# Four matmuls of 128 columns and two levels of sums in place of four matmuls of 256 columns and one level, in the inverse stage of a spectral block

## The chip, the cores and the metric

One core of a Trainium2 chip. The metric is the device time of the whole program in microseconds (us), on the slowest core, which here is the only one. In the profiles PE is TensorE's matmul, PEld its weight load, DVE VectorE, ACT ScalarE, POOL GpSimd and SP the queue that issues loads and stores.

## The reference, cut to what matters

```python
# A: normalise rows, 2-D real FFT (2048 x 512), multiply by W, inverse FFT
h  = x + irfft2(rfft2(layernorm(x)) * (w_r + 1j * w_i))
# B: normalise again, squared-ReLU MLP (512 -> 1792 -> 512), residual
r  = relu(layernorm(h) @ w1 + b1)
h2 = h + (r * r) @ w2 + b2
```

The 2048 rows lie as 16 groups of 128. The transforms are matmuls with sine and cosine tables. The change touches the last transform, which turns 257 complex frequencies into the 512 columns of a group.

## The kernel before: the parts that the change touches

For a group g, `s5` makes the even part of the output (256 columns of the table for lt = 0 and 2) and the odd part (lt = 1 and 3). `s5b` adds and subtracts them to the 512 columns R, by the symmetry of sine and cosine about the middle. `s6` multiplies by the row transform KI. `s6a` and `s6b` add x and take row statistics. Comments are mine.

```python
def s5(g, ahead=False):
    pe = bank("p5", "po", 2) if ahead else bank("p5", "pp", 3)
    for e in range(2):
        for r in range(2):
            lt = 2 * r + e
            nc.tensor.matmul(pe[:, 256 - 256 * e:512 - 256 * e],
                             lhsT=T2[:, lt, g].rearrange("p q s -> p (q s)"),
                             rhs=GI[:, lt, :], start=(r == 0), stop=(r == 1))
    def rest():
        od = ffn.tile([P, 256], FP32, tag="od", bufs=4, name="od")
        nc.scalar.copy(od[:], pe[:, 256:512])        # ACT: one half of PSUM to SBUF
        Rs[g] = pe, od
    ...
def s5b(g):                                          # DVE: two adds of 256 fp32, one side PSUM
    pe, od = Rs[g]
    Rs[g] = R = ffn.tile([P, 512], BF16, tag="R", bufs=3, name="R")
    nc.vector.tensor_tensor(R[:, 0:256], pe[:, 0:256], od[:], ALU.add)
    nc.vector.tensor_tensor(R[:, 256:512], pe[:, 0:256], od[:], ALU.subtract)
```

The groups are normalised and sent through the MLP in five chunks. While the MLP of chunk c runs ("loop c"), the pieces of chunk c+1 are dealt between its slots. A slot is one `up` of four matmuls or one `down` of four or five. Which slot a piece follows is decided when the program is built, by a counter of estimated PE time:

```python
CHUNKS = ((0, 2), (2, 5), (5, 9), (9, 13), (13, 16))

def prep_steps(c, total):                            # pieces of chunk c: (time, cost, piece)
    ...
        if k >= 2:
            steps.append((t, 0.22, lambda g=a + k - 2: s6(g)))
        if k < n:
            steps.append((t, 0.44, lambda g=a + k: s5(g)))
        if 1 <= k <= n:
            steps.append((t + 0.1, 0, lambda g=a + k - 1: s5b(g)))
        if k >= 2:
            steps.append((t + 0.1, 0, lambda g=a + k - 2: (s6a(g), s6b(g, on_act(c, g)))))
    t = t0 + (n + 1) * gap
    steps.append((t + 1.6, 0, lambda: rstd(c)))
    steps.append((t + 2.2, 0, lambda: norm(c)))
    steps.append((total - 2.4, 0.12 * n, lambda: transp(c, 0)))
    steps.append((total - 1.7, 0.12 * n, lambda: transp(c, 1)))

def run(c):
    ...
        prep = prep_steps(c + 1, sum(t for t, _ in slots) + 0.9 * n)
    for k, (t, slot) in enumerate(slots):
        slot()
        at += t
        while prep and (prep[0][0] <= at or k == len(slots) - 1):
            _, cost, piece = prep.pop(0)
            piece()
            at += cost
```

The 0.9 a group is 0.44 (s5) + 0.22 (s6) + 0.24 (transposes). Every engine then keeps this order.

## Time and profile before

| | before |
|---|---|
| time, median of 3 | 172.66 us (172.52 to 172.68) |
| span of the profiled run | 170.8 us |
| PE busy | 157.6 us, 92% |
| DVE busy | 123.6 us, 72% |
| ACT busy | 106.3 us, 62% |
| s5 in the loops | 4 x 256 columns, 0.44 us of PE a group |
| s5b in the loops | 2 adds, 0.66 us of DVE a group from start to start |

### The profile page before, as it was taken

How to read it: one execution, taken by the hardware profiler on the slowest of the kernel's cores; microseconds unless marked ns; L12 is line 12 of the kernel's file. 1: busy time of each engine (PE TensorE's matmuls, PEld its weight loads, DVE VectorE, ACT ScalarE, POOL GpSimd, SP SyncE). 2: the span in 40 equal slices, each digit the busy share in tenths (PEclk: the TensorE clock that was granted, in tenths of full speed). 3: DMA queues.
4: the chain of work that ended last, by engine and by line, in shares of the span. 5: the costliest groups of instructions: out<-in, count | busy, mean ns of one | idle time of the engine just before them, and what ended most of it. 6: DMA issues, size and time to landing. Idle time of an engine off the chain costs nothing.

```text
span 170.8 us, 2709 instructions
## 1 busy us (share of the span) xinstructions
PE 157.6 (92%) x967; PEld 92.4 (54%) x981; DVE 123.6 (72%) x287; ACT 106.3 (62%) x188; POOL 36.7 (22%) x63
## 2 busy tenths in 40 slices
PE   3988797999989899899999999999999999999992
PEld 1455565887854774456445444544544454556461
DVE  6998678979956698668997577498567577578320
ACT  3999785898976772288653677245387434478200
POOL 7788900000000003134000235000034200025000
PEclk9999999999999999999999999999999999999999
DMA  5994999992000000100000100000100001010011
GB/s 165 326 281 83 223 152 272 387 241 26 0 0 0 4 0 2 55 12 0 0 31 31 35 0 2 0 31 31 35 30 0 0 31 33 25 38 0 0 60 34
DMA packets 12621, 11.42 MB, mean 67 GB/s; under 512 B 6976, under 2 KB 11072, under 8 KB 12608
## 3 DMA queue, kind: packets, MB, share of 16 engines
q1 hardware_dynamic: 12448, 10.33, 22.6%
q0 software_dynamic: 160, 0.92, 1.9%
q8 instruction: 7, 0.11, 0.3%
q14 instruction: 6, 0.05, 0.1%
HBM read 8.01 MB, written 2.10 MB: 59 GB/s over the span
## 4 chain that ended last, share of the span: by engine, by line
PE 72%; DVE 16%; ACT 5%; issue 2%; POOL 2%; DVEq 0%; POOLq 0%; ACTq 0%
PE ph L688 29%; PE po L721 25%; DVE st L215 3%; PE p L542 3%; PE p L344 3%; ACT U L361 2%; PE po L709 2%; PE p L643 2%; PE p L587 1%; PE idle L259 1%; POOL rs L222 1%; DVE KFr L226 1%; DVE mA L419 1%; ACT X L391 1%; DVE mB L419 1%
## 5 line engine op out<-in xcount | busy, mean ns | idle before, releaser
L688 PE MATMUL ph<-UT,W 128*128 128x384 bf16 (+2 forms) x278 | 49.8, 336 | 1.6 <-DVE UT L774 0.6
L691 ACT ACTIVATE rl<-ph,b1f 128x384 bf16<-128x384 f32 (+2 forms) x70 | 41.5, 602 | 13.7 <-PE ph L688 10.6
L721 PE MATMUL po<-W,act 128*128 128x512 bf16 x203 | 48.1, 379 | 0.4
L692 DVE TENSOR_TENSOR act<-rl 128x384 bf16<-128x384 bf16 (+2 forms) x70 | 34.2, 514 | 15.4 <-ACT rl L691 14.9
L688 PEld LDWEIGHTS <-W 128*128 128x128 bf16 x280 | 27.3, 98 | 22.9 <-issue 2.1
L695 POOL TENSOR_TENSOR hb<-hs,b2b 128x512 f32<-128x512 bf16 x16 | 18.4, 1153 | 98.2 <-DVE act L692 98.2
L721 PEld LDWEIGHTS <-act 128*128 128x128 bf16 x210 | 20.4, 98 | 21.8
L725 DVE TENSOR_TENSOR ot<-po,hb 128x512 bf16<-128x512 f32 x15 | 10.3, 688 | 9.3 <-PE po L721 8.0
L591 DVE SCALAR_TENSOR_TENSOR hs<-p,xs 128x512 bf16<-128x512 f32 x15 | 10.3, 684 | 1.2 <-PE p L587 0.9
L259 PE MATMUL p<-ones 128*128 128x512 bf16 x22 | 8.1, 516 | 2.9 <-POOL ones L152 2.9
L546 ACT COPY od<-p 128x256 f32<-128x256 f32 x14 | 5.1, 370 | 7.9 <-PE p L542 7.9
L647 ACT COPY UT<-p 128x768 bf16<-128x768 bf16 (+1 forms) x4 | 3.6, 906 | 9.4 <-PE p L643 9.4
L542 PE MATMUL p<-GI,T 128*128 128x256 bf16 x56 | 8.2, 272 | 0.4 <-DVE hs L591 0.2
L259 PEld LDWEIGHTS <-ones 128*128 128x128 bf16 x40 | 4.4, 112 | 7.6 <-POOL ones L152 2.9
L602 ACT ACTIVATE junk<-hs 128x512 bf16<-128x512 bf16 x6 | 3.8, 630 | 7.6 <-DVE hs L591 7.6
L344 PE MATMUL p<-GF,Bt 128*128 128x256 bf16 x64 | 8.3, 273 | 0.0
L577 DVE TENSOR_TENSOR R<-p,od 128x256 bf16<-128x256 f32 x15 | 6.2, 415 | 2.4 <-ACT od L561 1.3
L215 DVE BATCH_NORM_STATS2 st<-xs 128x6 f32<-128x512 bf16 x12 | 7.8, 676 | 0.0
L542 PEld LDWEIGHTS <-T 128*128 128x128 bf16 x56 | 5.4, 97 | 3.5 <-issue 1.2
L473 ACT CAST T<-p 128x1024 bf16<-128x1024 f32 x7 | 7.2, 1025 | 0.0
L344 PEld LDWEIGHTS <-Bt 128*128 128x128 bf16 x64 | 6.1, 98 | 1.4 <-DVE Bt L251 0.4
L605 DVE BATCH_NORM_STATS2 st<-hs 128x6 f32<-128x512 bf16 x9 | 6.3, 695 | 0.3
(177 smaller groups left out, 226.0 us busy)
## 6 DMA issues: line engine op xcount, KB each, us to landing
W<-in_B_w_dram SPq DMA_DIRECT2D x2, 1792.0 KB, 10.3
out_dram<-ot SPq DMA_DIRECT2D x15, 128.0 KB, 1.8
xs<-in_A_x_dram SPq DMA_DIRECT2D x3, 512.0 KB, 6.5
WB<-in_A_w_r_dram SPq DMA_DIRECT2D x1, 578.2 KB, 6.0
WB<-in_A_w_i_dram SPq DMA_DIRECT2D x1, 578.2 KB, 7.2
xs<-in_A_x_dram SPq DMA_DIRECT2D x2, 256.0 KB, 3.3
b2b<-in_B_b_dram SPq DMA_DIRECT2D x1, 128.0 KB, 8.7
out_dram<-ot SPq DMA_DIRECT2D x2, 64.0 KB, 1.9
```

Source lines behind the costliest of these rows:

```text
L215: nc.vector.bn_stats(st[:], xs[:, g, :])
L259: nc.tensor.matmul(o, lhsT=ones[:, 0:P], rhs=ones[:], start=True, stop=True)
L344: nc.tensor.matmul(puv[:, :, e, :], lhsT=Bt[:, 2 * t + 1 - e, 2 * pr + q, :], rhs=GFv[:, t, :, e, :], start=(t == 0), stop=(t == 1))
L473: nc.scalar.copy(dst, src[0])
L542: nc.tensor.matmul(pe[:, 256 - 256 * e:512 - 256 * e], lhsT=T2[:, lt, g].rearrange("p q s -> p (q s)"), rhs=GI[:, lt, :], start=(r == 0), ...
L591: nc.vector.scalar_tensor_tensor(hs[:, g, :], Ys.pop(g)[:], WSC, xs[:, g, :], ALU.mult, ALU.add)
L688: nc.tensor.matmul(ph[:, 0:n], lhsT=W1[:, d, bass.ts(f, P)], rhs=UT[:, d, 0:n], start=(d == 0), stop=(d == ND - 1))
L691: nc.scalar.activation(rl[:, 0:n], ph[:, 0:n], ACT.Relu, bias=b1f[:, f:f + 1], scale=1.0)
L692: sq = nc.vector.tensor_tensor(act[:, f, 0:n], rl[:, 0:n], rl[:, 0:n], ALU.mult)
L695: add = nc.gpsimd.tensor_tensor(hb[:, g, :], hs[:, g, :], b2b[:], ALU.add)
L721: nc.tensor.matmul(po[:], lhsT=act[:, f, bass.ts(i, P)], rhs=W2[:, f, :], start=(f == 0), stop=(f == NF - 1))
L725: nc.vector.tensor_tensor(ot[:], po[:], hb[:, g, :], ALU.add)
```

## The change

The intent is to halve the PE work of `s5`. Sine and cosine are symmetric once more about the quarter, so 128 columns of each of the four tables are enough. They are no longer accumulated but kept apart, and a first level of sums on DVE (H) makes the even and odd parts. ACT copies all 512 columns to bfloat16 (V), and the four columns without a partner (two of each part) to H. Groups 0 and 1, which come first, keep their old way. The table gets 128 more columns. The counter charges 0.22 for s5. One of the two copies made ahead moves into loop 0.

```diff
     def s5(g, ahead=False):
-        for e in range(2):
-            for r in range(2):
-                lt = 2 * r + e
-                nc.tensor.matmul(pe[:, 256 - 256 * e:512 - 256 * e], lhsT=T2[:, lt, g]..., rhs=GI[:, lt, :],
-                                 start=(r == 0), stop=(r == 1))
+        for lt, tb, o in ((1, GI[:, 1, 0:129], 0), (3, GI[:, 3, 1:128], 129), (0, GI[:, 0, 0:128], 256),
+                          (2, GIa[:, 1024:1152], 384)):
+            nc.tensor.matmul(pe[:, o:o + tb.shape[1]], lhsT=T2[:, lt, g]..., rhs=tb, start=True, stop=True)
         def rest():
-            nc.scalar.copy(od[:], pe[:, 256:512])
-            Rs[g] = pe, od
+            nc.scalar.copy(V[:].rearrange("p e h c -> p (e h c)"), pe[:])
+            nc.scalar.copy(H[:, :, 0:129:128], pe[:]...[:, :, :, 0])
+            Rs[g] = V, H
     def s5b(g):
+        nc.vector.tensor_tensor(H[:, :, 1:128], V[:, :, 0, 1:128], V[:, :, 1, 1:128], ALU.add)
+        nc.vector.tensor_tensor(H[:, :, 255:128:-1], V[:, :, 0, 1:128], V[:, :, 1, 1:128], ALU.subtract)
+        nc.vector.tensor_tensor(Rv[:, 0::3], he, ho, ALU.add)
+        nc.vector.tensor_tensor(Rv[:, 2:0:-1], he, ho, ALU.subtract)
@@ prep_steps
-        steps = []
+        steps = [(0.4, 0, rest[1])] if c == 1 else []
-                steps.append((t, 0.44, lambda g=a + k: s5(g)))
+                steps.append((t, 0.22, lambda g=a + k: s5(g)))
... (the tiles V and H, three buffers each; group 0's old sums; the wider table GIa and its angles;
     rest[0] before the first transposes: cut)
```

The total of 0.9 a group in `run` was left as it was.

More of the change, by code (lines that the diff above doesn't have):

```diff
@@ L80 @@
     KI = persist.tile([P, P], BF16, name="KI")
-    GI = persist.tile([P, 4, 256], BF16, name="GI")
+    GIa = persist.tile([P, 1152], BF16, name="GIa")
+    GI = GIa[:, 0:1024].rearrange("p (t c) -> p t c", t=4)
     GIn = persist.tile([P, 2, 256], BF16, name="GIn")
@@ L140 @@
     fiE = [tab.tile([P, 9 * P], I32, name=f"fiE{i}") for i in range(2)]
-    fiI = tab.tile([P, 1024], I32, name="fiI")
+    fiI = tab.tile([P, 1152], I32, name="fiI")
     nc.gpsimd.iota(pI[:, 0:1], pattern=[[0, 1]], base=0, channel_multiplier=1)
@@ L327 @@
                                 float(HT if lt // 2 else QT), ALU.mult, ALU.add)
+    nc.gpsimd.memset(idxD[:, 0:1], 384)
+    nc.gpsimd.tensor_scalar(fiI[:, 1024:1152], idxD[:, 0:P], cols[:, 4:5], float(HT), ALU.mult, ALU.add)
     def cos_negs():
@@ L511 @@
         if pr == 5:
-            sin_of(GI[:].rearrange("p t c -> p (t c)"), fiI[:])
-            nc.scalar.activation(GIn[:], fiI[:].bitcast(I16)[:, ::2].rearrange("p (t c) -> p t c", t=4)[:, 0::2, :],
+            sin_of(GIa[:], fiI[:])
+            nc.scalar.activation(GIn[:], fiI[:, 0:1024].bitcast(I16)[:, ::2].rearrange("p (t c) -> p t c", t=4)[:, 0::2, :],
                                  ACT.Sin, scale=-SIN_SCALE)
@@ L538, in s5 @@
         pe = bank("p5", "po", 2) if ahead else bank("p5", "pp", 3)
-        for e in range(2):
-            for r in range(2):
-                lt = 2 * r + e
-                nc.tensor.matmul(pe[:, 256 - 256 * e:512 - 256 * e], lhsT=T2[:, lt, g].rearrange("p q s -> p (q s)"),
-                                 rhs=GI[:, lt, :], start=(r == 0), stop=(r == 1))
-        def rest():
-            od = ffn.tile([P, 256], FP32, tag="od", bufs=4, name="od")
-            nc.scalar.copy(od[:], pe[:, 256:512])
-            Rs[g] = pe, od
+        for lt, tb, o in ((1, GI[:, 1, 0:129], 0), (3, GI[:, 3, 1:128], 129), (0, GI[:, 0, 0:128], 256),
+                          (2, GIa[:, 1024:1152], 384)):
+            nc.tensor.matmul(pe[:, o:o + tb.shape[1]], lhsT=T2[:, lt, g].rearrange("p q s -> p (q s)"), rhs=tb,
+                             start=True, stop=True)
+        def rest():
+            V = ffn.tile([P, 2, 2, 128], BF16, tag="V", bufs=3, name="V")
+            H = ffn.tile([P, 2, 256], BF16, tag="H", bufs=3, name="H")
+            nc.scalar.copy(V[:].rearrange("p e h c -> p (e h c)"), pe[:])
+            nc.scalar.copy(H[:, :, 0:129:128], pe[:].rearrange("p (e h c) -> p e h c", e=2, h=2)[:, :, :, 0])
+            Rs[g] = V, H
         if ahead:
@@ L576, in s5b @@
         Rs[g] = R = ffn.tile([P, 512], BF16, tag="R", bufs=3, name="R")
-        nc.vector.tensor_tensor(R[:, 0:256], pe[:, 0:256], od[:], ALU.add)
-        nc.vector.tensor_tensor(R[:, 256:512], pe[:, 0:256], od[:], ALU.subtract)
+        if g == 0:
+            nc.vector.tensor_tensor(R[:, 0:256], pe[:, 0:256], od[:], ALU.add)
+            nc.vector.tensor_tensor(R[:, 256:512], pe[:, 0:256], od[:], ALU.subtract)
+            return
+        V, H = pe, od
+        nc.vector.tensor_tensor(H[:, :, 1:128], V[:, :, 0, 1:128], V[:, :, 1, 1:128], ALU.add)
+        nc.vector.tensor_tensor(H[:, :, 255:128:-1], V[:, :, 0, 1:128], V[:, :, 1, 1:128], ALU.subtract)
+        Rv = R[:].rearrange("p (k c) -> p k c", k=4)
+        he, ho = (H[:, e].rearrange("p (k c) -> p k c", k=2) for e in range(2))
+        nc.vector.tensor_tensor(Rv[:, 0::3], he, ho, ALU.add)
+        nc.vector.tensor_tensor(Rv[:, 2:0:-1], he, ho, ALU.subtract)
     def s6(g):
@@ L769 @@
         nc.vector.tensor_scalar(u2[:, g, :], hs[:, g, :], mv2[:, g, 0:1], rs2[:, g:g + 1], ALU.subtract, ALU.mult)
+    rest[0]()
     for g, cp in ((0, nc.scalar.copy), (1, nc.vector.tensor_copy)):
@@ L774 @@
         cp(UTs[0][:, :, P * g:P * g + P], pt[:, 0:ND * P].rearrange("p (d c) -> p d c", d=ND))
-    for r in rest:
-        r()
     s5b(2)
```

## The prediction

> **What bounds the kernel now.** I read the page's busy shares first, then the chain that ended last, then busy time by stretch, then the order of time on DVE in one stretch. The page, parts 1 and 4:
> ```profile
> PE   157.6 (92%) x967; PEld 92.4 (54%) x981; DVE 123.6 (72%) x287; ACT 106.3 (62%) x188; POOL 36.7 (22%) x63
> ...
> PE 72%; DVE 16%; ACT 5%; issue 2%; POOL 2%; DVEq 0%; POOLq 0%; ACTq 0%
> ```
> From about 60 us on, the chain is PE: the MLP's matmuls (L688, L721) with the inverse stage of the next row groups dealt in between. The kernel treats the 16 groups as five chunks (2, 3, 4, 4, 3); I call the MLP of chunk c "loop c". During loops 0 to 3 the code emits the pieces of chunk c+1 (s5, s5b, s6, s6ab, rstd, norm, two transposes) when a running cost counter passes set times. Every engine keeps that emission order. So PE stands whenever one of its pieces needs a DVE result that is not there yet. Busy time by stretch (columns PE, PEld, DVE, ACT, POOL, clock, DMA share, GB/s); these three hold the prep of loops 1, 2 and 3:
> ```profile
> 84.00:94.00 10.00, 9.74 (x59) 5.10 (x59) 8.57 (x20) 4.94 (x12) 0.00 (x0) 1.00 0.08 26
> ...
> 108.00:122.00 14.00, 13.74 (x81) 7.22 (x82) 11.08 (x25) 5.87 (x15) 0.00 (x0) 1.00 0.09 29
> ...
> 134.00:149.00 15.00, 14.95 (x84) 7.52 (x83) 9.63 (x22) 6.26 (x16) 0.07 (x1) 1.00 0.06 19
> ```
> PE loses only 0.26, 0.26 and 0.05 us there: PE bounds, and DVE is just behind it. How closely shows in DVE's order of time:
> ```profile
> 84.12 0.41 DVE L577 TENSOR_TENSOR R<-p,od 128x256 bf16<-128x256 f32 x1
> 84.46 0.41 DVE L578 TENSOR_TENSOR R<-p,od 128x256 bf16<-128x256 f32 x1
> 84.79 0.68 DVE L591 SCALAR_TENSOR_TENSOR hs<-p,xs 128x512 bf16<-128x512 f32 x1
> 85.50 0.69 DVE L605 BATCH_NORM_STATS2 st<-hs 128x6 f32<-128x512 bf16 x1
> 86.23 0.18 DVE L606 BATCH_NORM_AGGREGATE mv<-st 128x2 f32<-128x6 f32 x1
> 86.33 0.39 DVE L577 TENSOR_TENSOR R<-p,od 128x256 bf16<-128x256 f32 x1
> ```
> No idle time is noted before any of these: from 82.6 to 89.9 DVE runs without a gap. And in the chain, the end of that loop:
> ```profile
> 88.31 4.10 PE po L721 x19
> 92.41 0.89 PE p L643 x16
> 93.31 0.05 issue
> 93.36 0.81 PE po L721 x3
> ```
> The 16 transposes take 0.89 us, and a last down slot (0.81) follows and hides the copies of their result. DVE's normalised rows were ready at 91.95, only about 0.3 us ahead of the transposes at 92.25.
>
> **What the Trainium skill says.** "TensorE: Matmul & The Clock Gate", section Back-to-back issue gap, gives 55.8 ns for an isolated 128-column matmul and some 81 ns where every one loads weights. The trace decides: the 16 transposes, each with its own weights and 128 columns, come every 0.89/16 = 56 ns. "Vector Engine (DVE) Microarchitecture Reference", section 5.1, lets a two-source add of 2-byte operands handle two elements a cycle at an innermost step of plus or minus one, and says that 4-byte alignment made no difference when checked; how a negative step streams it calls not measured. The trace agrees on alignment: the spectral products read W from column 1 of rows of 257, aligned in odd rows only, and yet all sixteen have one duration:
> ```profile
> L419 DVE TENSOR_TENSOR mA<-X,WB x8: 684/689/695, 23.6 to 45.0; 128x1024 bf16<-128x1024 bf16 x8
> L419 DVE TENSOR_TENSOR mB<-X,WB x8: 685/688/691, 24.2 to 45.6; 128x1024 bf16<-128x1024 bf16 x8
> ```
> "Perfetto Trace Analysis", section DVE / Act Engine Instruction, says that a profiled duration runs to the write's acknowledgement while the next instruction may begin earlier. The trace agrees: 0.41 us adds start 0.33 apart (84.12, 84.46, 84.79); the batch statistics, which need the result before them, start after the full 0.68. I count starts, not durations.
>
> **The change, part by part.** *PE*: s5 had four matmuls of 256 columns, 0.44 us a group in the chain. Now it has 129+127+128+128 columns: four times 56 ns, 0.22. It saves 0.22 a group. Groups 4 to 15 lie in the loops: 12 x 0.22 = **-2.6 us**. Groups 2 and 3 run before the loops, in the chain ahead of the idle matmuls (8 matmuls, 0.87 us): **-0.4**, as the inputs of the first transposes (DVE, about 55.1) are ready by the earlier time.
>
> *ACT*: the copy of 256 columns (370 ns) becomes one of 512 (like L572, 587 ns) plus a four-element copy, estimated at 190 ns from the accumulator reads: +0.4 us a group. ACT has room in the later loops; in loop 0 its ReLUs take 0.41 per 0.44 us of PE, so two such sets there delay it. The bank of s5 comes free after ACT, before DVE, so PSUM gets easier.
>
> *DVE*: the two adds from PSUM, 2 x 0.33 = 0.66 us of engine time a group, become four from SBUF: two of 254 elements and two of 256. At two a cycle I put each at 282 ns, as the squares of 128x256 are, starting 0.20 apart (three squares in 0.66 us). The third needs the second's result: 0.20+0.32+0.20+0.20 = 0.92, **+0.26 a group**. If odd rows or the backward write drop the first pair to one a cycle (411 ns), it is 0.33+0.45+0.20+0.20 = 1.18, +0.52.
>
> *Emission*: the cost counter now takes 0.22 for s5, while the stage's total keeps 0.9 a group. So pieces fall later among the slots. Stepping the counter by hand: in loops 1 and 2 both transposes now come after the last down slot, in loop 3 the second one does. The copy of the first half (ACT, 1.01 us) then stands open: about 1.05 - 0.45 (the second half's transposes) = 0.6 us in loops 1 and 2, some 0.3 to 0.6 in loop 3.
>
> *Loop 1, worked*: times from its first matmul (71.80). Between the end of the last square and R of group 8, DVE before ran from 11.06 to 15.17 = 4.11 us. After, three more s5b cost 0.78 and an output add (0.61) now precedes the last s5b: 4.11+0.78+0.61 = 5.5, begun at 10.8, so R(8) at 16.4. PE arrives at s6(8) earlier by four s5: 15.8-0.2-0.9 = 14.7. It stands **1.7 us**; before, it didn't. With 0.6 for the open copy and 0.9 saved, the stall less the small ones of before leaves loop 1 about **+0.8** longer.
>
> *Loop 2*, same way from its first down slot (106.3): R(12) at 10.0 because a statistics pair and an output add lie ahead of it; PE there at 8.7; stall 1.4, plus 0.6, less 0.9, less old idle 0.2: **+0.9**. *Loop 3*: stalls 0.5 at s6(13), 0.5 at s6(15), some 0.6 at the transposes (the last normalisation moves back by the same lag), copy 0.3 to 0.6, less 0.7: **+1.2**. *Loop 0*: DVE is already full from 56 to 68 us; ACT's two new sets and three s5b of +0.26 cost about 0.7, against 0.5 from the earlier start: **+0.2**. *Loop 4* has no prep: 0.
>
> Sum: 0.2+0.8+0.9+1.2 = +3.1. All waits in my steps are taken as hard; each loop has a small slack (buffers three deep, DVE gaps of 0.2 to 0.3) that I can't place. I take off 0.5: **+2.6 us, 175.3 us**.
>
> **Rivals.** (1) *PE bound throughout*: only PE's term counts, 172.66-3.0 = 169.7, less the open copies (+1.5): 171. For it: DVE is busy 72%, and easier PSUM. Against: the unbroken DVE stretch and the 0.3 us lead before the transposes. (2) *The slow pair*: one element a cycle, +0.26 more for each of 14 groups, nearly all on the path by then: some 1.5 to 3 us more, about 177. For it: row length 127, the step of -1 that no instruction of this trace has. Against: the odd-aligned products at full rate. (3) *DVE hidden, the emission shift alone bites*: -3.0 plus 1.5 plus small stalls: within 1 us of before. (4) *ACT the bound*: its load in windows 2 and 3 is half of PE's, so only in loop 0.
>
> **Range and chances.** Rivals 1 and 3 give 171 to 173, the main line 174.5 to 176, rival 2 up to 178. Eight in ten: 172.6 to 177.4. Faster than 169.2 would need more than PE's whole saving: 0.02. Slower than 176.1 needs the main line with little slack or rival 2: 0.30. Within 2%: 0.68.
>
> **What would show it right or wrong.** In the profile after: s5 groups of four at 0.22 us; the s5b adds at 282 ns (or 411 for the first two); new PE idle before L587's successor of s5b (s6, waiting for R) of over 1 us in each of loops 1 and 2; PE idle of 0.5 us before the first up matmul of loops 2 and 3 waiting for UT; DVE gapless in those prep stretches. If PE's waits in the loops sum to less than 2 us, my lag is wrong, and the time falls below 173. If the adds take 411 ns, the time goes over 176.

## More of the kernel before

The view of waits for PE in the kernel before, from 55 us to the end (columns: who waited, for what; us in total, times, longest):

```profile
PE ph L688 <- DVE UT L774: 0.6, 1, 0.6
PE ph L688 <- ACT UT L647: 0.6, 1, 0.6
PE ph L688 <- ACT rl L691: 0.4, 1, 0.4
PE p L542 <- DVE hs L591: 0.2, 1, 0.2
```

In over 110 us the view lists four waits of PE, 1.8 us in all. Apart from the first, at the start of loop 0, these are three small waits.

## The result, and the profile after

The changed kernel took 179.51 us (178.70 to 179.67, 4 runs), the kernel before 172.67 us in the same rounds. The ratio is 1.0385, with a 95% interval of 1.0351 to 1.0419: slower. A ratio here is the mean time of one kernel's fast runs over that of the other's of the same rounds, so it is not quite the ratio of the medians quoted. The prediction said 175.3, with 172.6 to 177.4 as its range.

Part 1 of the page after; DVE's busy share went down a point while PE lost four:

```profile
PE   156.9 (88%) x981; PEld 90.3 (51%) x981; DVE 126.3 (71%) x315; ACT 109.8 (62%) x202; POOL 37.2 (21%) x65
```

The view of waits for PE after, again from 55 us to the end:

```profile
PE p L606 <- DVE R L597: 4.2, 4, 1.6
PE ph L707 <- ACT UT L666: 1.9, 3, 0.7
PE ph L707 <- ACT rl L710: 1.4, 2, 1.2
PE p L662 <- DVE u L650: 0.8, 1, 0.8
PE ph L707 <- DVE UT L668: 0.6, 1, 0.6
PE ph L707 <- DVE UT L794: 0.6, 1, 0.6
```

1.8 us of waits have become 9.5. The first line is `s6` waiting for R, the second and fifth the first `up` of a loop waiting for a copy of the transposed rows, the fourth the transposes waiting for normalised rows. Busy time by stretch, for the stretches that hold the prep of loops 1 to 3 (columns as in the prediction):

```profile
84.00:97.00 13.00, 10.71 (x67) 5.47 (x68) 11.08 (x30) 5.78 (x15) 0.00 (x0) 1.00 0.07 24
113.00:126.00 13.00, 10.94 (x69) 5.58 (x68) 11.22 (x30) 5.78 (x15) 0.00 (x0) 1.00 0.10 32
141.00:156.30 15.30, 12.47 (x71) 5.69 (x69) 9.65 (x26) 5.96 (x17) 0.00 (x0) 1.00 0.08 27
```

PE now stands for 2.3, 2.1 and 2.8 us of these. In the first two DVE is busier than PE. PE's order of time at the end of loop 1 shows both kinds of wait:

```profile
89.84 0.38 PE L606 MATMUL p<-R,KI 128*128 128x512 bf16 x1 [1.64 <-DVE R L597]
...
95.02 1.06 PE L662 MATMUL p<-ident,u 128*128 128x128 bf16 x16
96.73 12.25 PE L707 MATMUL ph<-UT,W 128*128 128x512 bf16 x56 [0.65 <-ACT UT L666]
```

Before, a down slot lay between the transposes of loop 1 and the next loop's matmuls; now nothing does. A group's `s5` on PE, before and after (matmuls overlap; the next one starts 0.43 and 0.23 us after the first of these):

```profile
78.30 0.60 PE L542 MATMUL p<-GI,T 128*128 128x256 bf16 x4
```

```profile
79.57 0.39 PE L548 MATMUL p<-GIa,T 128*128 128x129 bf16 x4
```

What is new per group on DVE:

```profile
84.04 0.28 DVE L592 TENSOR_TENSOR H<-V 128x254 bf16<-128x254 bf16 x1
84.24 0.28 DVE L593 TENSOR_TENSOR H<-V 128x254 bf16<-128x254 bf16 x1
84.56 0.29 DVE L596 TENSOR_TENSOR R<-H 128x256 bf16<-128x256 bf16 x1
84.77 0.28 DVE L597 TENSOR_TENSOR R<-H 128x256 bf16<-128x256 bf16 x1
84.97 0.68 DVE L610 SCALAR_TENSOR_TENSOR hs<-p,xs 128x512 bf16<-128x512 f32 x1
```

Four sums in 0.93 us from the first start to the next instruction's, at two elements a cycle although the first pair starts at an odd column and one of them writes backwards.

The lengths of the loops say where the time went. A loop runs from its first `up` matmul to that of the next, loop 4 to the end of the span; "start" is the time of the first `up`. The second column of the changed kernel is a repeat (experiment 10 below).

| profiled run | start | loop 0 | loop 1 | loop 2 | loop 3 | loop 4 | span |
|---|---|---|---|---|---|---|---|
| before | 56.66 | 15.14 | 22.21 | 27.98 | 27.13 | 21.68 | 170.8 |
| changed, first | 56.99 | 16.09 | 23.65 | 29.21 | 29.21 | 22.45 | 177.6 |
| changed, again | 56.32 | 16.10 | 23.66 | 29.22 | 29.20 | 22.40 | 176.9 |
| old order, new sums (1) | 57.08 | 15.96 | 22.15 | 28.00 | 27.92 | 21.59 | 172.7 |
| new order, old sums (2) | 56.66 | 15.35 | 23.03 | 29.07 | 28.95 | 22.44 | 175.5 |
| new order, transposes early (9) | 56.66 | 14.82 | 22.41 | 28.44 | 28.95 | 21.62 | 172.9 |
| total follows (6) | 56.51 | 16.10 | 23.89 | 27.99 | 26.97 | 21.64 | 173.1 |
| old order, no first sums (7) | 56.59 | 15.34 | 21.01 | 26.83 | 26.45 | 21.58 | 167.8 |
| old matmuls, bf16 sums (4) | 56.81 | 14.88 | 21.67 | 27.67 | 26.97 | 21.60 | 169.6 |

### The profile page after: what moved, and what is told of

The parts are those of the page before. It is cut to its first block, busy times and chain, and to the rows that moved or that the text cites. A ratio compares the mean times of both kernels' runs of the same rounds, so it can differ in the third digit from the quotient of the medians.

```text
span 177.6 us, 2783 instructions
## 1 busy us (share of the span) xinstructions
PE 156.9 (88%) x981; PEld 90.3 (51%) x981; DVE 126.3 (71%) x315; ACT 109.8 (62%) x202; POOL 37.2 (21%) x65
## 5 line engine op out<-in xcount | busy, mean ns | idle before, releaser
L707 PE MATMUL ph<-UT,W 128*128 128x384 bf16 (+2 forms) x280 | 50.4, 336 | 4.5 <-ACT UT L666 1.9
L740 PE MATMUL po<-W,act 128*128 128x512 bf16 x210 | 48.9, 379 | 0.0
L554 ACT CAST V<-p 128x512 bf16<-128x512 f32 x14 | 8.1, 581 | 7.7 <-PE p L548 7.7
L606 PE MATMUL p<-R,KI 128*128 128x512 bf16 x15 | 5.7, 380 | 4.3 <-DVE R L597 4.2
L245 PE MATMUL p<-KFr,xs 128*128 128x256 bf16 x24 | 5.7, 278 | 1.0 <-DVE KFr L227 0.9
L365 ACT CAST U<-p 128x1024 bf16<-128x1024 f32 x6 | 6.2, 1029 | 0.3 <-PE p L348 0.3
```

Source lines behind the costliest of these rows:

```text
L554: nc.scalar.copy(V[:].rearrange("p e h c -> p (e h c)"), pe[:])
L707: nc.tensor.matmul(ph[:, 0:n], lhsT=W1[:, d, bass.ts(f, P)], rhs=UT[:, d, 0:n], start=(d == 0), stop=(d == ND - 1))
L740: nc.tensor.matmul(po[:], lhsT=act[:, f, bass.ts(i, P)], rhs=W2[:, f, :], start=(f == 0), stop=(f == NF - 1))
```

## The experiments

The theory: PE's saving is real, but two things eat it. The sums on DVE are longer, and the pieces stand in another order because the counter charges less; both make `s6`, the transposes and the next loop wait. Rivals: A, the longer sums alone; B, the order alone; C, ACT's two copies. The first two experiments part the two causes, each against the kernel before.

**1. New sums, old order.** One number in the changed kernel:

```diff
-                steps.append((t, 0.22, lambda g=a + k: s5(g)))
+                steps.append((t, 0.44, lambda g=a + k: s5(g)))
```

> The changed kernel with one number put back: the step of four 128-column matmuls counts 0.44 again in the emission counter, so the pieces fall between the same MLP slots as before the change. Theory (DVE lag plus the shifted order, both needed): the three open copies of the transposed rows go (about 0.65 us each) and the last sums of a chunk no longer stand behind an output add; what stays is some 0.3 us of DVE per group: 173.5 to 175.5 us. Rival A (longer sums alone make the loss, order is harmless): 178 to 180. Rival B (order alone makes it): 169.5 to 171.5, the whole saving of PE.

Measured: 174.72 us, ratio 1.0121 (1.0092 to 1.0149), correct. As the theory said. Rivals A and B both fall: putting the order back gives most of the loss back, but not all. (The copy that moved into loop 0 stays there in this kernel; it was not moved back by itself.)

**2. Old sums, new order.** The same number in the kernel before, the other way (0.44 to 0.22).

> The kernel before with one number changed: its step of 256-column matmuls counts 0.22, so the pieces fall as in the changed kernel. Theory: the open copies show without any new work on DVE: +1.5 to +2.2 us, 174 to 175. Rival A (order harmless): within 0.5 us of before. Rival B (order alone): 178 to 180.

Measured: 177.30 us, ratio 1.0260 (1.0239 to 1.0281), correct. Neither theory nor rival had it: the order alone costs 4.5 us, two to three times what I had counted, with not one instruction changed. PE's waits for DVE and ACT in this run:

```profile
PE ph L688 <- ACT UT L647: 1.9, 3, 0.7
PE p L587 <- DVE R L578: 1.0, 3, 0.4
PE p L643 <- DVE u L631: 0.9, 1, 0.9
PE ph L688 <- DVE UT L649: 0.6, 1, 0.6
PE ph L688 <- DVE UT L774: 0.6, 1, 0.6
PE ph L688 <- ACT rl L691: 0.6, 1, 0.6
```

All kinds of wait of the changed kernel are there; those for R (1.0 against 4.2) and for ReLUs (`rl`, 0.6 against 1.4) are shorter. With 1.9 us for the new matmuls and sums (experiment 1) and 4.5 for the order, the two add to 6.4; together they cost 6.1 to 6.8 (the lower figure is that of experiment 10). So they hardly help or hinder each other.

**3. The changed kernel without the first-level sums** (wrong, relative error 0.031):

```diff
-        nc.vector.tensor_tensor(H[:, :, 1:128], V[:, :, 0, 1:128], V[:, :, 1, 1:128], ALU.add)
-        nc.vector.tensor_tensor(H[:, :, 255:128:-1], V[:, :, 0, 1:128], V[:, :, 1, 1:128], ALU.subtract)
-        he, ho = (H[:, e].rearrange("p (k c) -> p k c", k=2) for e in range(2))
+        he, ho = V[:, 0], V[:, 1]
```

> The changed kernel without the two first-level sums (wrong result on purpose): two adds of 256 per group on DVE, 0.41 us in place of 0.96, all copies, matmuls and the order as changed. Theory (DVE's length): the waits of the inverse matmul for R in loops 1 to 3 go, the open copies stay: 170.5 to 173. Rival C (the two copies on ACT, 0.75 us a group, are what delays): 177 to 179, hardly moved.

Measured: 174.92 us, ratio 1.0117 (1.0095 to 1.0138). Some 4 us came back, which speaks against C, but it missed the expected range on the slow side: PE's waits for R fell to 0.7 us, while those for UT (1.9), for the normalised rows (0.9) and for the second half's copy (0.6) stayed. They belong to the order.

**7. The same without the first-level sums, in the old order** (wrong). The edits of 1 and 3 together.

> The changed kernel without its two first-level sums (wrong result on purpose) and with the old order: new matmuls, new copies, DVE at 0.41 us a group. Theory (PE's saving is real and DVE's length eats it in the old order): 169.5 to 171, that is 2 to 3 us under before. Rival C (ACT's two copies stand in the way): 172 or more.

Measured: 169.52 us, ratio 0.9819 (0.9804 to 0.9834): 3.0 us faster than before, so C falls. That this equals PE's saving as predicted (2.6 in the loops, 0.4 ahead) is in part luck, as DVE's work on the sums is also shorter here than before (0.41 for 0.66 us). The nearer comparison is experiment 4 below, which has this shorter DVE work with the old matmuls (it lacks ACT's second copy and the copy moved into loop 0, too): against it (ratio 0.9922) the new matmuls with their copies bring 1.8 us. By the table that is 2.0 us in loops 1 to 3, where 11 x 0.22 = 2.4 were counted, and some 0.3 before the loops once the load of x is taken out, less 0.46 lost in loop 0, where PE waits 0.6 us for ReLUs beside ACT's two copies and experiment 4 lists no such wait. Of the sums and the order either alone is enough to lose more than PE saves: by the ratios this kernel loses 5.2 us by the first-level sums (experiment 1) and as much by the order (experiment 3).

**9. The new order with the transposes put back.** In experiment 2's kernel, the transposes' two times are 0.9 us earlier. Stepping the counter shows that in loops 1 to 3 nothing else changes place; in loop 0 the transposes move as well.

```diff
-        steps.append((total - 2.4, 0.12 * n, lambda: transp(c, 0)))
-        steps.append((total - 1.7, 0.12 * n, lambda: transp(c, 1)))
+        steps.append((total - 3.3, 0.12 * n, lambda: transp(c, 0)))
+        steps.append((total - 2.6, 0.12 * n, lambda: transp(c, 1)))
```

> The kernel before in the new order (177.3, 4.5 us over before), but with the transposes' two times 0.9 us earlier, so that they come before the last down slot again and nothing else changes place in loops 1 to 3. Theory: the open copies (0.65 us each in loops 1 and 2) and the wait for the second half behind an output add in loop 3 (0.6 or more) go: 175.0 to 175.8. The rest, over 2 us, is waits of the inverse matmul and of loop 3's transposes. If the transposes' place is all of it: 173. If it is nothing: 177.

Measured: 174.72 us, ratio 1.0126 (1.0100 to 1.0151), correct: just under the expected range. 2.6 us came back. By the table: 0.6 in each of loops 1 and 2 (the open copy), 0.8 at the start of loop 4 (the second half's copy), and 0.5 in loop 0, which I had not counted. Loop 3 kept its 28.95.

**8. Why loop 3 is long.** DVE's order of time in the changed kernel (first profile) at the end of loop 3:

```profile
151.89 0.18 DVE L641 RECIPROCAL rs<-sd 128x3 f32<-128x3 f32 x1 [2.15 <-ACT sd L638]
152.00 0.69 DVE L744 TENSOR_TENSOR ot<-po,hb 128x512 bf16<-128x512 f32 x1
152.60 1.05 DVE L650 TENSOR_SCALAR u<-hs,mv,rs 128x512 bf16<-128x512 bf16 x3
155.07 0.69 DVE L744 TENSOR_TENSOR ot<-po,hb 128x512 bf16<-128x512 f32 x1 [1.41 <-issue]
155.68 0.55 DVE L668 COPY UT<-p 128x768 bf16<-128x768 bf16 x1
```

DVE sits idle for 2.15 us behind a reciprocal that waits for ACT's statistics of the last group (so it does in the kernel before, at 146.37), and then an output add stands ahead of the normalisation, because the new order has a down slot between `rstd` and `norm`. Later a second add stands ahead of the copy of the second half. In experiment 2's kernel I had `norm` emitted with `rstd` (time t + 1.6), which by the counter moves it in loop 3 alone.

> The kernel before in the new order (177.3), with the normalisation emitted together with the reciprocal, which changes places only in loop 3, where an output add stood between them. Theory: that add (0.6 us) leaves the path of the transposes: 176.4 to 176.9. If the transposes waited for the statistics alone: 177.2 or more.

Measured: 177.06 us, ratio 1.0260 (1.0244 to 1.0276), correct. By its time this is undecided: the ratio is that of experiment 2. In the trace loop 3 went from 28.95 to 28.45 us and the transposes' wait from 0.9 to 0.4, as meant. So the add was worth 0.5 us. The larger part of loop 3's loss is put down to the last `s6`, one down slot later in the new order, and the chain of statistics behind it. The traces fit: from the start of this `s6` to the first transpose it is 5.39 us in the kernel before (142.03 to 147.42) and 5.30 in the changed one (147.77 to 153.07), so a later `s6` means later transposes. But no run here moved it alone.

**6. The total follows the cost.** In the changed kernel:

```diff
-            prep = prep_steps(c + 1, sum(t for t, _ in slots) + 0.9 * n)
+            prep = prep_steps(c + 1, sum(t for t, _ in slots) + 0.68 * n)
```

> The changed kernel with its stage total at 0.68 a group in place of 0.9, so that the counter agrees with the 0.22 it now charges; the transposes come before the last down slot again in every loop. Theory (the order is the larger loss, through transposes and output adds that change places): 173.5 to 175.5, about as good as the changed sums in the old order (174.7). Rival (only the exact old order is good): 177 or more.

Measured: 174.85 us, ratio 1.0138 (1.0118 to 1.0158), correct. One constant that agrees with the other gives 4 us back. Loops 2 and 3 are then as short as before; loops 0 and 1 are not, and in loop 1 `s6` of group 7 waits for R longest, 1.65 us. So the exact old order is not needed, but the sums' length remains.

**5. The wider table alone.** The kernel before plus `GIa` with 1152 columns and its angles, unused.

> The kernel before plus the changed kernel's wider table (1152 columns in place of 1024, two more small POOL instructions), which nothing reads. In the three profiles with this table x landed some 0.6 us later than in the three without. If the table (its place in memory, or the larger program) does that: +0.5 to +0.9 us. If those were chance: +0.1 us, the table's own sine.

Measured: 172.68 us, ratio 1.0007 (0.9993 to 1.0021), correct. The table costs nothing that can be seen.

**10. The changed kernel again.**

> The changed kernel unaltered, a second time, to size the start: in its first profile x landed 0.65 us later than in the profiles of before. If that was chance of the load: x at about 6.4 to 6.8 us and 178.7 to 179.2 this time. If it belongs to this program: x at 7.3 us again and 179.5.

Measured: 178.74 us (178.73 to 178.95), ratio 1.0351 (1.0328 to 1.0374). The load of W waits for the third block of x, so its issue shows when x landed. First profile, then this one (the queue's order of time):

```profile
7.25 0.33 SPq L112 DMA_DIRECT2D WB<-in_A_w_r_dram  x1
```

```profile
6.40 0.33 SPq L112 DMA_DIRECT2D WB<-in_A_w_r_dram  x1
```

In the kernel before it was 6.44. The loops agree to 0.1 us between the two profiles, so of the first 6.8 us some 0.7 belong to a late load and not to the change. (Not in every run: in one of the first four the span was 177.0 us, and the rest of its 179.64 lay outside it; another took 178.70.) The change's own cost is nearer 6.1 us.

**4 and 12. Old matmuls, all 512 columns to bfloat16.** The part of the change that spares DVE, without the rest:

```diff
-            od = ffn.tile([P, 256], FP32, tag="od", bufs=4, name="od")
-            nc.scalar.copy(od[:], pe[:, 256:512])
-            Rs[g] = pe, od
+            V = ffn.tile([P, 512], BF16, tag="V", bufs=4, name="V")
+            nc.scalar.copy(V[:], pe[:])
+            Rs[g] = V[:, 0:256], V[:, 256:512]
```

The two sums then read V.

> The kernel before with its own matmuls and order, but ACT copies all 512 columns to bfloat16 (0.58 us in place of 0.37) and DVE's two sums read these (0.41 us a group in place of 0.66). Theory (DVE's length sets PE's small waits): 0.3 to 1.0 us faster than before. Rival C (ACT's copy sets it): 0.5 us or more slower.

> The version with old matmuls and bfloat16 sums again, beside the mixed one on the same chip, with more rounds: 0.6 to 1.0 per cent faster than before (171.0 to 171.6).

Measured: 171.37 us, ratio 0.9922 (0.9895 to 0.9949), and again 171.43 us, ratio 0.9922 (0.9905 to 0.9939), correct both times. This beats both kernels, and by 1.3 to 1.5 us, more than the first expectation's 1.0. The sums from PSUM (413 ns) become sums from SBUF at 285 ns, 0.20 us apart; ACT's copy grew from 370 to 585 ns and nothing waits for it on PE. Of PE's four waits from 55 us on that the view listed before, only the first two are left. The two that went are 0.6 us; the rest of the gain that view doesn't show. Three things changed at once: the type, the memory that DVE reads, and when the bank of PSUM comes free (now after ACT, before after DVE); no run parts them.

**11. Mixed.** The version of 4, with the four 128-column matmuls and both levels of sums for groups 5, 9 and 13 only, in the old order, since DVE had idle time by their sums.

> The version with old matmuls and bfloat16 sums (171.4), where groups 5, 9 and 13 alone take the four 128-column matmuls and the two levels of sums, in the old order. DVE has idle time beside the sums of these groups, so theory expects 3 times 0.22 us of PE less: 170.6 to 171.0. If DVE's lag carries on to the end of a loop instead: 171.4 or more.

Measured: 171.78 us, ratio 0.9943 (0.9926 to 0.9960), correct. It missed, and the rival's figure came: not faster than 171.43 beside it. By its trace loop 2 (group 9) gained 0.22 us, as it should, but loops 1 and 3 grew by 0.24 and 0.30, with two new waits:

```profile
PE p L614 <- DVE R L602: 0.6, 2, 0.3
```

DVE's idle time lies beside the sums of groups 5 and 13 but is not enough before the next `s6`. In these two profiles the loops also start 0.27 us later, 0.16 of it with the load of x (issue of W at 7.09 against 6.93).

## Why the prediction was wrong

Right, by its own steps:

- PE: 0.22 us a group, as the trace has it. As time, experiment 7 against experiment 4 shows 1.8 of the 3.0 us counted.
- DVE: four adds of 282 to 292 ns at two elements a cycle; rival 2 (the slow pair) did not come. I put the set at 0.92 us; the trace has 0.93 to 1.00.
- The waits and their places, as idle time that the profile lists: at R(8) 1.7 us predicted and 1.64 measured, at R(12) 1.4 and 1.41, the open copies 0.6 and 0.65, in loop 3 0.5, 0.5 and 0.6 against 0.54, 0.64 and 0.82.
- The start: -0.4 predicted, -0.34 in the repeat.

Wrong: the sum. The mechanism held, and the step that failed is the one that turned waits into loop lengths. Of the 3.5 us by which +2.6 fell short of +6.1, 1.6 lie in loop 3 and the start of loop 4, 0.65 in loop 1, 0.5 in the slack taken off, 0.4 in the start and loop 0, and 0.3 in loop 2.

| | predicted | measured (repeat less before) | waits less saving, with refills |
|---|---|---|---|
| start and loop 0 | +0.2 | -0.34 + 0.96 | -0.3 + 1.0 |
| loop 1 | +0.8 | +1.45 | +1.4 |
| loop 2 | +0.9 | +1.24 | +1.2 to +1.5 |
| loop 3 and start of loop 4 | +1.2 | +2.07 + 0.72 | +2.6 |
| "small slack" | -0.5 | 0 | |
| sum | +2.6 | +6.1 | |

First, **a wait costs more than the idle time that the profile lists**. A matmul of 512 columns lasts 379 ns in the trace, but in a stream they start every 215 ns (five take 1.24 us). "TensorE: Matmul & The Clock Gate" of the Trainium skill, section Single matmul latency, gives (398 + N)/2.4 ns for a single warm matmul, which is 379 ns for N = 512. The trace has the same figure, but the profile models the ends of matmuls, so this does not test the page; the starts are measured. I had read the page and used only its rate. So each stop of PE costs its listed idle time plus some 0.16 us, a "refill" below. In the changed kernel the five matmuls ahead of s6(8) begin at 86.96; in a stream s6 would have followed 5 x 0.215 later, at 88.04; it began at 89.84, 1.80 us late, where the view has 1.64.

The prediction's stalls were worked as R's time less PE's arrival, so its 1.7 is to be held against this 1.80. It came of two readings that were both some 0.3 us early: s6(8) stood at 16.13 before (87.93 less 71.80), not at 15.8, and R(8) was there at 16.7, not 16.4. That it fits is in part luck.

With refills the loops come out. For loop 3 and the start of loop 4: 0.54 + 0.64 + 0.82 + 0.64 of waits, four refills of 0.16, less 0.66 saved: 2.6; measured 2.8. For loop 1: 1.65 + 0.65, one stop more than before, less the old 0.2 and 0.88 saved: 1.4; measured 1.45. For loop 0: 1.36 of waits for ReLUs against 0.35, one stop more, less 0.22: 1.0; measured 0.96. I had put it at 0.7, and on ACT's copies as much as on the sums. But before the longest of these waits ACT itself stood idle, 1.43 us, for a square of DVE, and with the same copies and no first-level sums loop 0 is 0.6 us shorter (15.34 in experiment 7, 15.96 in experiment 1): most of it is DVE again.

Second, **loop 3 was mis-sized**. Every one of its four waits was taken too short, the transposes' most (0.6 for 0.82), as I had not seen that the output add stands between reciprocal and normalisation (0.5 us in experiment 8); and the copy of the second half was given as "0.3 to 0.6" in place of 0.64 plus a refill. In loop 1 my own terms (1.7 + 0.6 - 0.9) make 1.4; writing "+0.8" took off small waits that the kernel before hardly had.

Third, **0.5 us were taken off for a slack that I could not place**. No run shows any.

Fourth, the change was read as "DVE lag, plus a shift". Rival 3, the shift alone, counted 1.5 us of open copies and "small stalls" for it. Measured alone it costs 4.5 us (experiment 2), more than twice the net 1.9 us of matmuls and sums. The number that was not changed, the total of 0.9 a group, matters as much as the one that was: experiment 6 changes it and gives 4 us back.

The time (179.5) also holds about 0.8 us over the repeat, in the profiled run a late load, which nothing in the kernel explains; without it the range would still have been missed (178.7 against 177.4).

Left open: how much of loop 3's 1.8 us over before (experiment 9's kernel) is the last `s6` standing one slot later; and whether another order, made for the new sums, would bring them below 171.4 us. Experiments 1 and 6 are two orders of many.

## What to carry to other kernels

Where one engine is full and a second nearly so, work taken from the first and given to the second is paid for where the first waits for it: count each new stop of PE as its listed idle time plus a refill, here 0.16 us. An emission order made from cost estimates is part of the tuning, so after a change of one cost, step the counter again and keep its total in agreement; here one stale constant cost more than the arithmetic gained. And look for the half of a change that helps by itself: reading bfloat16 from SBUF in place of fp32 from PSUM was worth 0.8%, without the new matmuls. A control should differ from the run that it is held against in as little as can be: beside the kernel before, experiment 7 seemed to show the whole saving of the matmuls, beside experiment 4 it shows 1.8 us.

## What the Trainium skill lacked or had wrong

- "Vector Engine (DVE) Microarchitecture Reference", section 5.1, lists a negative step as not measured for how the engine streams it. Here a two-source bfloat16 subtraction of 2 x 127 elements that writes with a step of -1 took 287 ns, the add of the same size with a step of +1 282 ns, both from an odd start column: both at the two-a-cycle rate (the square of 256 elements takes 285 ns). The changed kernel's result is correct.
- The same page and "VectorE: DVE Perf Modes" differ on 4-byte alignment (the second asks for it). The runs side with the first: 684 to 695 ns for all sixteen products of 1024 elements, aligned or not, and the 282 ns above.
- "TensorE: Matmul & The Clock Gate" has the single matmul's latency and the stream's rate, and why a stream hides what a single one can't, but does not draw what follows for reading a bound PE's waits: that each costs some 0.16 us on top of the idle time that a profile lists (1.80 us for a listed 1.64; 379 ns against 215). With it the loops' lengths come out to 0.3 us.
- Its 81 ns for a 128-column matmul in a stream with weight loads is not seen here: four such matmuls with four weights start 57 ns apart, and the 16 transposes, each with its own weights, 56 ns apart. Nor is the 131 ns that the same sentence gives for 512 columns: 215 ns here.
- No page that I read says how much the start of a program may vary: the load that waits for the same 0.5 MB block of x was issued at 6.40 us and at 7.25 us in two runs of one kernel.
